# Linear attention, a channel mix and a gated mix in one kernel: plain split products in place of Strassen's, and a list scheduler's order

## The chip, the cores and the metric

The kernel runs on one core of a Trainium2 chip. The time is the device time of one execution in microseconds, shown as the median of three runs. A profile is one more execution with the hardware profiler on; its span runs from the first to the last instruction. TensorE multiplies into PSUM (eight banks), VectorE (DVE) and ScalarE (ACT) read and write PSUM and SBUF, GpSimd (POOL) works on SBUF, and SyncE (SP) issues the DMAs. Each engine takes its instructions in order.

## The reference, cut to what matters

All inputs are float32 or float64 arrays; batch B = 2, heads H = 8, sequence S = 768, head width 64, model width 512.

```
# 1 attention with decay, per head: state = gamma*state + k_t v_t^T ; y_t = scale * q_t state
# 2 token mix of rank 32 and channel mix
xt = x.transpose(0, 2, 1)
u  = x + (xt @ U @ V).transpose(0, 2, 1)
x  = u + np.maximum(u @ w_ch1, 0) @ w_ch2            # 512 -> 2048 -> 512
# 3 gated mix
h    = np.maximum(x @ w_in, 0)                       # 512 -> 1024
u, v = h[..., :512], h[..., 512:]
v_n  = (v - mean(v)) / sqrt(var(v) + 1e-6)           # over the 512 features
v_s  = einsum('ts,bsd->btd', w_spatial, v_n) + b_spatial[None, :, None]
out  = (u * v_s) @ w_out                             # 512 -> 512
```

The weights U, V, w_ch1, w_ch2, w_in and w_out reach the kernel as float64 words and are turned into float32 on the chip.

## The kernel before, in words

**Numbers.** A product of full float32 quality is made of three products of split operands. Each operand is a high part (rounded by ScalarE to the product's type) and the remainder (a subtraction on VectorE or GpSimd): high x high, high x low, low x high (`mm3`, all recorded under L129). An activation block is 128 features x 384 tokens, half of the sequence T = 384. X[b] holds the 512 features of a batch as four tiles of 128 partitions x 768 tokens.

**Attention** goes over eight units i, a pair of heads each (four pairs for batch 0, then four for batch 1), in chunks of 128 tokens. `scale_q`, `scale_k` apply decays. `s1(i)` makes the score products (two heads side by side on half of the array each, tile `sc`), their masking into `pt` (VectorE, or ScalarE and GpSimd), the chunk products k^T v (`ds`) and the running state `s` (VectorE, L226 to L228: ten small steps on the two diagonal blocks of a 128 x 128 tile whose other blocks are zero). `s2(i)` multiplies the states and the probabilities into `x` and copies it to X. `s3`, `s4`, `s5` do the token mix of rank 32: transposes (`t`), their split (`xtok`), the product with U (`g`, twelve products of 256 columns for two pairs), the product with V (`hu`) and the addition to X. These functions are called in an order written out by hand, the later steps of a unit behind the first steps of the next ones.

**Channel mix and gate** use Strassen's scheme in Winograd's form (`strassen`): four output blocks from seven products instead of eight. It needs sums of activation blocks (`form_diff`, L300; split by `form_split`, L292), sums of weight blocks (`sums1`, `sums2`, L472 to L478) and sums of product banks (`y`, L578 to L581, L645). The 2,048 inner features go in eight blocks m of 256: `ch1(m, b)` is one such quad with relu, `ch2(m, b)` multiplies its two inner tiles by w_ch2 into eight banks, and each bank is added to X by VectorE (L674). `ch1` of one block is woven with `ch2` of the block before. `mixu`, `mixv`, `mixo` are the gate's two halves and the output product, with Strassen; `norm` normalises v; `mixs` is the spatial product, plain, its bank multiplied into X (L758, L759). `mixv` and `mixo` have banks of 128 tokens x 256 columns, the others 128 x 384.

**Weights.** `load_next` loads a tile of 128 x 512 float64 words (512 KB) into one of two raw buffers. `conv_a` and `conv_b` make float32 of the words: two ScalarE operations (L366, L367), two on VectorE (L372, L373), one on GpSimd (L374); then the split. A small task queue (`pump`) starts and advances these steps at beats of the program.

**Order.** All instructions are issued in program order; some 300 choices found for this kernel (`CHOICES`: how many tasks begin at a beat, which engine takes a step, orders of products) set where a step stands.

The heart of the scheme:

```
order = pick(f"or{ycls(name)}", order)          # "1675243"
...
    elif x == "6":
        prod(qb, P6, True)
        nc.vector.tensor_add(y1, qb, y1)
    elif x == "7":
        prod(qc, P7, True)
        nc.vector.tensor_add(y2, qc, y1)
```

Of the kernel before, what the change touches and what calls it, by code (L numbers as in the profile page):

```python
# [10 lines left out]
U64 = mybir.dt.uint64  # L11
# [8 lines left out]
DFF2 = 1024  # L20
# [8 lines left out]
NM = NF // 2  # L29
# Beats (how many tasks begin), engines (A, V, G), orders of products and of steps, by point of the program.  # L30
CHOICES = {
# [54 lines left out]
def pick(key, default):  # L86
    """The schedule's choice at a point of the program, where it differs from the usual one."""
    return CHOICES.get(key, default)
# [986 lines left out]
```

## Time and profile before

| | |
|---|---|
| time, three runs | 532.05, 534.75, 538.35 us (median 534.75) |
| span of the profiled execution, first to last instruction | 530.7 us (the profile gives no other time of that execution) |
| TensorE busy, products | 479.1 us (90%), 3,157 |
| VectorE busy, instructions | 439.5 us (83%), 821 |
| ScalarE busy, instructions | 255.4 us (48%), 537 |
| GpSimd busy, instructions | 292.3 us (55%), 265 |
| mean granted TensorE clock | 0.957 of 2.4 GHz |
| HBM read, written | 39.79 MB, 3.15 MB |

Busy shares are means over the whole span. A matmul's length in the profile reaches from its start to the end of its results; successive ones overlap, so rates are read from the distance of starts. A float32 product of the attention is recorded as two instructions, a split product as one. The granted clock of a stretch is a mean over two levels, 1.2 and 2.4 GHz. The words "idle before" name the time in which an engine had nothing running before an instruction, with what released it.

### The profile page before, as it was taken

The page shows a single profiled execution, that of the slowest core. Times are in us where ns is not written, and L with a number is a line of the kernel's source. Part 1 is how long each engine was busy: PE and PEld are TensorE (multiplying, and loading weights), DVE is VectorE, ACT ScalarE, POOL GpSimd, SP SyncE. Part 2 cuts the span into 40 slices and gives each one's busy share as a digit, 9 for nine tenths or more (in the row PEclk, how much of TensorE's full clock was granted, in tenths as well). Part 3 has the DMA queues.
Part 4 walks back from the last instruction along what each step waited for, and adds up shares of the span by engine and source line. Part 5 has one row for each costly group of instructions (what it writes and reads, how often), then busy time and mean ns, then how long its engine had stood idle before and what let it go on. Part 6 is the DMA issues. An engine that isn't in the chain of part 4 may idle for free.

```text
span 530.7 us, 8624 instructions
## 1 busy us (share of the span) xinstructions
PE 479.1 (90%) x3157; PEld 456.0 (86%) x3157; DVE 439.5 (83%) x821; ACT 255.4 (48%) x537; POOL 292.3 (55%) x265
## 2 busy tenths in 40 slices
PE   6878778989888999999999999995899999999697
PEld 4667667979887999999999999883799889999697
DVE  3788899997978987697877878999986886799873
ACT  1575655535454555444544545355343664445220
POOL 2566865683595456554664544676744550476720
PEclk7988898999999999999999999996799999999799
DMA  7996220102322222102222111220001210200123
GB/s 262 315 345 242 93 81 1 41 1 79 120 79 81 80 79 79 50 32 81 79 81 79 51 67 46 78 69 30 1 0 62 90 46 35 80 0 1 40 97 105
DMA packets 17419, 43.50 MB, mean 82 GB/s; under 512 B 2144, under 2 KB 6880, under 8 KB 17376
## 3 DMA queue, kind: packets, MB, share of 16 engines
q1 hardware_dynamic: 17376, 42.94, 24.3%
q8 instruction: 25, 0.41, 0.3%
q14 instruction: 18, 0.15, 0.1%
HBM read 39.79 MB, written 3.15 MB: 81 GB/s over the span
## 4 chain that ended last, share of the span: by engine, by line
PE 47%; DVE 32%; ACT 6%; DMA 6%; issue 5%; POOL 3%; SPq 1%; POOLq 0%; DVEq 0%; ACTq 0%
PE acc L129 17%; DVE t L300 3%; DMA q<-in_qT 3%; DVE x L674 2%; DVE s L228 2%; DVE fb L292 1%; DVE sm L722 1%; DVE pz L758 1%; DMA rawV<-in_V 1%; ACT r L736 1%; DVE x L759 1%; DVE rw L372 1%; DMA k<-in_kT 1%; DVE rw L373 1%; DVE ft L292 1%
## 5 line engine op out<-in xcount | busy, mean ns | idle before, releaser
L129 PE MATMUL acc<-a,hw 128*128 128x384 f32 x512 | 130.6, 335 | 2.0 <-DVE x L674 0.9
L129 PEld LDWEIGHTS acc<-a,hw 128*128 128x128 f32 x512 | 92.3, 188 | 3.2 <-DVE x L674 1.4
L129 PE MATMUL acc<-a,lw 128*128 128x384 f32 x256 | 85.6, 334 | 0.0
L674 DVE TENSOR_TENSOR x<-acc,x 128x384 f32<-128x384 f32 x128 | 68.8, 548 | 6.4 <-PE acc L129 6.4
L156 POOL TENSOR_TENSOR a<-y,a 128x384 fp32r<-128x384 f32 x41 | 42.5, 1042 | 55.4 <-ACT a L155 54.0
L374 POOL TENSOR_TENSOR rw<-rw,tw 128x512 int32<-128x512 int32 x32 | 41.2, 1287 | 47.5 <-DVE rw L373 28.8
L653 ACT ACTIVATE y<-y 128x384 f32<-128x384 f32 x42 | 22.1, 525 | 72.9 <-DVE y L645 72.9
L292 POOL TENSOR_TENSOR ft<-t,ft 128x384 fp32r<-128x384 f32 x33 | 37.6, 1149 | 30.0 <-ACT ft L288 29.8
L129 PEld LDWEIGHTS acc<-a,lw 128*128 128x128 f32 x256 | 48.0, 188 | 0.0
L288 ACT CAST ft<-t 128x384 fp32r<-128x384 f32 x48 | 23.2, 514 | 34.2 <-DVE t L300 34.2
L372 DVE TENSOR_SCALAR rw<-yw 128x512 uint32<-128x512 uint32 x32 | 28.6, 895 | 8.8 <-ACT yw L366 7.4
L292 POOL TENSOR_TENSOR fb<-x,fb 128x384 fp32r<-128x384 f32 x26 | 29.3, 1147 | 2.1 <-ACT fb L288 2.1
L373 DVE SCALAR_TENSOR_TENSOR rw<-yw,rw 128x512 uint32<-128x512 uint32 x32 | 26.5, 827 | 1.1
L129 PE MATMUL pz<-ws,vn 128*128 128x384 f32 x144 | 26.5, 335 | 0.1
L382 ACT CAST hw<-rw 128x512 fp32r<-128x512 f32 x16 | 10.0, 623 | 33.8 <-POOL rw L374 33.8
L129 PEld LDWEIGHTS pz<-ws,vn 128*128 128x128 f32 x144 | 25.1, 188 | 0.4 <-DVE vn L156 0.4
L366 ACT ACTIVATE yw<-raww 128x512 f32<-128x512 f32 x32 | 21.3, 667 | 2.3 <-DVE rw L372 2.3
L155 ACT CAST a<-y 128x384 fp32r<-128x384 f32 x42 | 21.6, 513 | 1.3
L367 ACT ACTIVATE tw<-raww 128x512 int32<-128x512 uint32 x32 | 21.1, 661 | 0.0
L129 PE MATMUL sc<-q,k 64*128 64x128 f32 x192 | 16.8, 324 | 4.3 <-DVE q L194 1.5
L129 PEld LDWEIGHTS sc<-q,k 64*128 64x128 f32 x192 | 14.7, 228 | 6.7 <-DVE q L194 2.7
L288 ACT CAST fb<-x 128x384 fp32r<-128x384 f32 x36 | 17.3, 512 | 4.9 <-DVE x L759 4.8
(1376 smaller groups left out, 1429.2 us busy)
## 6 DMA issues: line engine op xcount, KB each, us to landing
raww<-in_w SPq DMA_DIRECT2D x32, 512.0 KB, 3.6
kk<-in_k SPq DMA_DIRECT2D x8, 384.0 KB, 5.9
v<-in_v SPq DMA_DIRECT2D x8, 384.0 KB, 6.7
out_y<-o SPq DMA_DIRECT2D x24, 128.0 KB, 1.7
q<-in_qT SPq DMA_DIRECT2D x7, 384.0 KB, 5.9
k<-in_kT SPq DMA_DIRECT2D x7, 384.0 KB, 5.7
rawws<-in_ws SPq DMA_DIRECT2D x6, 384.0 KB, 3.1
rawwu<-in_wu SPq DMA_DIRECT2D x4, 512.0 KB, 4.0
```

What stands on the lines that cost most here:

```text
L129: nc.tensor.matmul(o, l, r, start=start, stop=stop, skip_group_check=True)
L155: nc.scalar.copy(hi, raw)
L156: eng.tensor_sub(lo, raw, f(hi))
L288: nc.scalar.copy(t[:, 0, :], blk[o])
L292: E(pick(f"f{b}{k}{o}{blks_gen[0]}", "V" if eng is V else "G")).tensor_sub(t[:, 1, :], blk[o], f(t[:, 0, :]))
L366: nc.scalar.activation(y, words[:, :, 1].bitcast(F32), AF.Copy, scale=2.0 ** -112)
L367: nc.scalar.activation(t, words[:, :, 0], AF.Copy, scale=2.0 ** -29)
L372: nc.vector.tensor_single_scalar(r, y.bitcast(U32), 3, ALU.logical_shift_left)
L373: nc.vector.scalar_tensor_tensor(r, y.bitcast(U32), 0x80000000, r, ALU.bitwise_and, ALU.bitwise_or)
L374: E(pick(f"cv{mcls(nm)}", "G")).tensor_tensor(r.bitcast(I32), r.bitcast(I32), t, ALU.add)
L653: nc.scalar.activation(y, y, AF.Relu)
L674: nc.vector.tensor_add(x, acc, x)
```

## The change

Strassen's scheme is gone: `ch1`, `gate_u`, `gate_v` and `final` are plain sums over four input tiles, three split products each (`triple`). The first channel product has eight products where there were seven; gate v and output make one bank of 128 tokens x 512 columns where there were 256 columns. The inner features go in four blocks of four tiles (GM = 4) instead of eight of two, so a bank of the second channel product sums twelve products instead of six and is added to X half as often. The state of the attention is kept as one 128 x 64 tile per chunk (both heads below each other, five steps instead of ten), and its product with q is two quarter-array products. Only one batch's channel mix begins before the other batch's attention: `AT0`, `AT1`, `CH0`, `CH1` give each step a key, the place that it would have in time in us. q and k are loaded in halves.

No step is issued where it stands in the program. `Plan.op` notes each with its key, the engines that could take it with a duration each, and what it reads and writes. `arrange` then goes through all steps: for each engine it takes, among the steps whose inputs are ready about as early as any (`SLACK`), the one with the lowest key, and gives buffers of the pools (`POOLS`: 36 tiles "a", 30 "w", 2 raw, 8 banks) in the order of the keys. `give_out` issues the result.

```diff
+    LAG = {"P": 198.0, "V": 35.0, "A": 35.0, "G": 35.0, "D": 30.0}
...
+        for _ in order:
+            best = None
+            for e in self.ENGINES:
+                can = []
+                for o in cands[e]:
+                    t0 = room(o)
+                    if t0 is not None:
+                        can.append((o.seq, o, t0) + span(o, e, t0))
...
+                low = min(c[3] for c in can) + SLACK[e]
+                for _, o, t0, st, en in sorted(can, key=lambda c: c[0]):
+                    if st > low:
+                        continue
+                    if any(span(o, x, t0)[1] + BIAS[x] < en + BIAS[e] for x in o.eng if x != e):
+                        continue
+                    if best is None or st < best[0]:
+                        best = st, en, o, e
+                    break
...
+def pe(n, passes=1):
+    return passes * (10.8 + 0.4219 * n), False
+GM = 4
+NM = NF // GM
+POOLS = {"a": 36, "w": 30, "raw": 2, "y": 2, "t": 2, "r": 3, "s": 3, "sm": 2, "ps": 8}
+SLACK = {"P": 30.0, "V": 60.0, "A": 60.0, "G": 100.0, "D": 30.0}
+BIAS = {"V": 300.0, "G": 0.0, "A": 0.0}
+AT0, AT1, CH0, CH1 = 5.0, 42.0, 36.0, 24.0
...
+    def triple(o, start, stop, n, wh, wl, xh, xl, r, flip=False):
...
+                mm(o.t, wh(), xh(), start, False)
+                mm(o.t, wh(), xl(), False, False)
+                mm(o.t, wl(), xh(), False, stop)
+        op({"P": pe(n, 3)}, run, r=r, w=[o])
...
+    def ch1(b, h, i):
+        o = rows(f"c{b}{h}{i}", 0, "w1", i, b, h)
+        A[b, h, i] = t = Buf("a", [P, 2, T], F32R, f"a{b}{h}{i}")
+        op({"A": aps(T)}, lambda E: E.activation(t.t[:, 0, :], o.t, AF.Relu), r=[o], w=[(t, 0)])
+        op({"V": (560, False)}, lambda E: E.scalar_tensor_tensor(t.t[:, 1, :], o.t, 0.0, f(t.t[:, 0, :]), ALU.max, ALU.subtract), r=[o, (t, 0)], w=[(t, 1)])
+
+    def ch2(m, b, h, d):
...
+        for i in range(GM * m, GM * m + GM):
...
+            triple(o, i == GM * m, i == GM * m + GM - 1, T, ...)
+        op({"V": vps(T)}, lambda E: E.tensor_add(xs(b, d, h), o.t, xs(b, d, h)), r=[o, ("X", b, d, h)], w=[("X", b, d, h)])
...
+        grp = 12 * pe(T)[0] / 1000
+        at = [AT0 + 6.5 * i for i in range(NP)] + [AT1 + 9.0 * i for i in range(NP)]
+        for i in range(2 * NP):
+            load_qk(i, at[i] - 12)
...
+            load_kv(i, at[i] - 10)
+        weight_u(at[2] + 3)
...
+        t = CH0
+        for m in range(NM):
+            for b in range(B):
+                ch[m, b] = t
+                t += 16 * grp + (CH1 if (m, b) == (0, 0) else 0)
+        gu = t
+        for m in range(NM):
+            for i in range(GM):
+                weight("w1", GM * m + i, ch[m, 0] + i * grp - LEAD)
...
+        for b in (0, 1):
+            for what in ("uv", "vu")[b]:
...
+        for b in range(B):
+            for h in range(2):
+                for d in range(ND):
+                    spatial(b, h, d)
+                    plan.key += 1.5 * grp
+                    operand(2, b, d, h)
+        for b in range(B):
+            for c in range(NCH):
+                final(b, c)
+                plan.key += 12 * pe(DM)[0] / 1000
+        plan.arrange(POOLS)
```

## Rows read from the trace of the kernel before

**Rows 1.** Stretches: length, TensorE, loads, VectorE, ScalarE, GpSimd busy (instructions), clock, DMA, GB/s.

```profile
0.00:45.00 45.00, 34.53 (x355) 27.23 (x357) 30.62 (x74) 20.23 (x43) 22.27 (x28) 0.85 0.91 306
45.00:93.00 48.00, 38.01 (x400) 32.22 (x396) 44.74 (x98) 29.13 (x65) 32.40 (x29) 0.93 0.24 83
93.00:180.00 87.00, 78.04 (x440) 74.96 (x439) 76.45 (x124) 44.19 (x89) 56.55 (x47) 1.00 0.19 64
180.00:330.00 150.00, 150.00 (x867) 150.00 (x866) 121.13 (x205) 72.10 (x140) 78.65 (x69) 1.00 0.21 69
330.00:390.00 60.00, 48.45 (x235) 44.54 (x234) 57.86 (x87) 28.76 (x61) 41.40 (x35) 0.86 0.12 40
390.00:465.00 75.00, 72.75 (x489) 71.13 (x488) 57.97 (x146) 39.59 (x96) 29.71 (x34) 1.00 0.16 55
465.00:510.00 45.00, 40.08 (x249) 39.15 (x249) 40.30 (x68) 17.91 (x40) 29.13 (x26) 0.92 0.07 24
510.00:525.00 15.00, 14.95 (x124) 14.70 (x124) 9.20 (x22) 3.15 (x8) 2.17 (x2) 1.00 0.33 106
```

**Rows 2.** Timeline of TensorE, 49 to 67 us: start, length, operation, idle time before it.

```profile
49.51 0.88 PE L129 MATMUL x<-pt,v 128*64 128x128 f32 x12
...
53.47 0.80 PE L129 MATMUL ds<-v,kk 128*64 128x64 f32 x20
54.20 0.87 PE L254 MATMUL t<-shared,x 128*128 128x128 f32 x6
54.91 0.61 PE L129 MATMUL x<-q,s 128*128 128x128 f32 x4
55.45 0.88 PE L129 MATMUL x<-pt,v 128*64 128x128 f32 x12
56.26 0.94 PE L129 MATMUL x<-q,s 128*128 128x128 f32 x6
57.12 0.88 PE L129 MATMUL x<-pt,v 128*64 128x128 f32 x12
57.93 0.39 PE L129 MATMUL g<-xtok,ust 128*128 128x256 f32 x1
61.88 2.71 PE L129 MATMUL g<-xtok,ust 128*128 128x256 f32 x11 [3.57 <-DVE xtok L256]
64.53 1.82 PE L129 MATMUL sc<-q,k 64*128 64x128 f32 x24
66.28 0.80 PE L129 MATMUL ds<-v,kk 128*64 128x64 f32 x20
```

**Rows 3.** Timeline of the end of the span: last product and last VectorE instruction.

```profile
527.01 0.28 PE L129 MATMUL qo5d<-hwo3c,fb 128*128 128x256 f32 x1
...
527.33 0.42 DVE L771 TENSOR_TENSOR o<-qo5d,yo 128x256 f32<-128x256 f32 x1 [0.29 <-PE qo5d L129]
```

**Rows 4.** Groups of instructions by line: count, busy us, mean ns, idle time before.

```profile
L129 PE MATMUL acc<-a,hw 128*128 128x384 f32 x512 | 130.6, 335 | 2.0 <-DVE x L674 0.9 <-DVE y L645 0.8 <-POOL a L156 0.3
...
L674 DVE TENSOR_TENSOR x<-acc,x 128x384 f32<-128x384 f32 x128 | 68.8, 548 | 6.4 <-PE acc L129 6.4
...
L366 ACT ACTIVATE yw<-raww 128x512 f32<-128x512 f32 x32 | 21.3, 667 | 2.3 <-DVE rw L372 2.3
...
L372 DVE TENSOR_SCALAR rw<-yw 128x512 uint32<-128x512 uint32 x32 | 28.6, 895 | 8.8 <-ACT yw L366 7.4 <-POOL lw15c L386 1.4
...
L373 DVE SCALAR_TENSOR_TENSOR rw<-yw,rw 128x512 uint32<-128x512 uint32 x32 | 26.5, 827 | 1.1
...
L374 POOL TENSOR_TENSOR rw<-rw,tw 128x512 int32<-128x512 int32 x32 | 41.2, 1287 | 47.5 <-DVE rw L373 28.8 <-ACT tw L367 15.1 <-PE acc L129 3.5
...
L228 DVE SCALAR_TENSOR_TENSOR s<-s,scales,ds 64x64 f32<-64x64 f32 x64 | 17.9, 280 | 2.1
...
L186 ACT ACTIVATE kk<-kk,scales 128x384 f32<-128x384 f32 x16 | 9.0, 615 | 10.2 <-DMA kk<-in_k 10.2
```

**Rows 5.** Waits of TensorE: us in total, times, longest.

```profile
PE qo0a L129 <- DVE yo L575: 4.4, 1, 4.4
```

More of the change, by code (lines that the diff above doesn't have):

```diff
@@ L1 @@
+import heapq
 from contextlib import ExitStack
@@ L19 @@
 DFF = 2048
-DFF2 = 1024
 R = 32
@@ L28, with __init__ @@
 TC = NCH // 2
-NM = NF // 2
-CHOICES = {
[51 rows of a table removed]
-}
-def pick(key, default):
-    return CHOICES.get(key, default)
-WARM = 11
-VIA = {i: (1, 3) for i in range(2, 8)}
-NW = 25
-EPS = 1e-6
-P1, P6, P7, P5 = ("a11", "b11"), ("s2", "t2"), ("s3", "t3"), ("s1", "t1")
-P2, P4, P3 = ("a12", "b21"), ("a22", "t4"), ("s4", "b22")
+EPS = 1e-6
+class Buf:
+    def __init__(self, pool, shape, dt, name):
+        self.pool, self.shape, self.dt, self.name = pool, shape, dt, name
+        self.t, self.left, self.end, self.order = None, 0, 0.0, None
@@ L101, in tile_kernel @@
+BIAS = {"V": 300.0, "G": 0.0, "A": 0.0}
+WARM = 11
+AT0, AT1, CH0, CH1 = 5.0, 42.0, 36.0, 24.0
+LEAD = 25.0
+VIA = {i: (1, 3) if i >= 2 else () for i in range(2 * NP)}
 @with_exitstack
@@ L204, in s1, with run @@
+        ds = bank([P, NCH - 1, D], f"ds{i}")
+        def run(_):
+            for c in range(NCH - 1):
                 for e in range(2):
                     r = slice(64 * e, 64 * e + 64)
[L206 to L215 removed]
@@ L246, in s3, with cpy, turn @@
+    def cpy(e, o, i):
+        (e.copy if e is nc.scalar else e.tensor_copy)(o, i)
+    def turn(i):
         b, p = divmod(i, NP)
@@ L268, in s5, with run @@
-    def s5(i):
+                xtok[j, h] = [Buf("a", [P, TC, 2 * P], F32R, f"xtok{j}{h}{y}") for y in range(2)]
+            hi, lo = xtok[j, h]
+            tr = bank([P, TC, P], f"t{i}{h}")
+            def run(_, tr=tr, h=h):
+                for c in range(TC):
+                    nc.tensor.transpose(tr.t[:, c, :], X[b][:, p, (TC * h + c) * P:(TC * h + c + 1) * P], ident)
+            op({"P": (TC * 111, False)}, run, r=[("X", b, p, h), "ident"], w=[tr])
+            sl = slice(w * P, (w + 1) * P)
@@ L525, in begin @@
-    def begin(stages, tasks):
-        tasks.append(list(stages))
-        advance(tasks, len(tasks) - 1)
-    def pump(n=1, w=0, hold=False):
-        advance(flow)
-        if not hold:
-            advance(wflow)
-        for z in range(n + w):
-            if jobs and z < n:
-                begin(jobs.pop(0), flow)
-                continue
-            if hold or begun[0] == limit[0] or running[0] == most[0]:
-                return
-            if not nxt:
-                t = next(wtasks, None)
-                if t is None:
-                    return
-                nxt.append(t)
-            need, pair, stages = nxt[0]
-            if strict[0] and need > free[0] - sum(x[0] for y in wflow for x in y if isinstance(x, tuple)):
-                return
-            if pair and heavy[0]:
-                return
-            nxt.pop()
-            ends = [end_task]
-            if pair:
-                heavy[0] = True
-                ends = [heavy_end, end_task]
-            running[0] += 1
-            begun[0] += 1
-            begin(stages + ends, wflow)
@@ L679, in weave @@
-    def weave(gens, pattern, beat):
-        for g in pattern:
-            next(gens[g])
-            beat()
-    def mixu(m, b):
-        def store(i, h, src, add=None, y=None):
-            if add is not None:
-                nc.vector.tensor_add(y, src, add)
-                src = y
-            if pick(f"ur{m}{b}{i}{h}", "A") == "A":
-                nc.scalar.activation(X[b][:, 2 * m + i, h * T:(h + 1) * T], src, AF.Relu)
-            else:
-                nc.vector.tensor_single_scalar(X[b][:, 2 * m + i, h * T:(h + 1) * T], src, 0.0, ALU.max)
-            if (b, i, h) == (1, 0, 1):
-                free[0] += 7
-        yield from strassen(f"u{m}{b}", T, ys3(f"u{m}{b}"), rows("wu", m, b), store)
@@ L699, in tile_kernel @@
-    vn, rv, vs = {}, {}, []
-    def mixv(g):
-        b, c = divmod(g, TC)
-        r = [st([P, DM], F32, f"r{g}{h}") for h in range(2)]
-        def store(i, h, src, add=None, y=None):
-            if add is not None:
-                nc.vector.tensor_add(y, src, add)
-                src = y
-            nc.scalar.activation(r[h][:, i * 2 * P:(i + 1) * 2 * P], src, AF.Relu)
-            if (i, h) == (0, 1):
-                vs.append(norm(g))
-        rv[g] = r, psm.tile([P, 2, 16], F32, tag="sm", name=f"sm{g}", bufs=2)
-        yield from strassen(f"v{g}", DM // 2, ys2(f"v{g}", pw, "w"), cols("wv", b, c * P), store, copy=nc.vector.tensor_copy)
@@ new lines, in final, with busy, run @@
+    def final(b, c):
+        o = chunk(f"o{b}{c}", 2, "wo", b, c)
+        t = Buf("w", [P, DM], F32, f"out{b}{c}")
+        op({"A": aps(DM), "V": vps(DM)}, lambda E: cpy(E, t.t, o.t), r=[o], w=[t])
+        dma(lambda: out[b, c * P:(c + 1) * P, :], lambda: t.t[:], P * DM * 4, r=[t])
+    with tc.manual_schedule():
+        warm = nc.const_aps.tensor(1.0, (P, T), BF16)
+        nc.scalar.activation(psm.tile([P, 1], F32, name="table"), warm[:, 0:1], AF.Copy)
+        idle = bank([P, T], "idle")
+        def busy(n):
+            def run(_):
+                for _ in range(n):
+                    mm(idle.t, warm[:, 0:P], warm, True, True)
+            op({"P": (n * 320.0, False)}, run, w=[idle])
+        plan.key = 0.0
+        busy(WARM)
+        grp = 12 * pe(T)[0] / 1000
+        at = [AT0 + 6.5 * i for i in range(NP)] + [AT1 + 9.0 * i for i in range(NP)]
+        for i in range(2 * NP):
+            load_qk(i, at[i] - 12)
+            if i == 0:
+                dma(lambda: ident, lambda: a["ident"], P * P * 4, w=["ident"], key=at[0] - 10)
+            load_kv(i, at[i] - 10)
+        weight_u(at[2] + 3)
+        weight_v(0, at[2] + 3.1)
+        weight_v(1, at[2] + 3.2)
+        for i in range(2 * NP):
+            plan.key = at[i] - 2
+            scale(i)
+            plan.key = at[i]
+            scores(i)
+            plan.key = at[i] + 5
+            mix(i)
+            plan.key = at[i] + 7
+            turn(i)
+            if i % 2:
+                plan.key = at[i] + 8
+                down(i // 2)
+                plan.key = at[i] + 9
+                up(i - 1)
+                up(i)
+        ch = {}
+        t = CH0
[7 more added lines that the diff above has]
+                weight("w1", GM * m + i, ch[m, 0] + i * grp - LEAD)
+            for i in range(GM):
+                weight("w2", GM * m + i, ch[m, 0] + (8 + i) * grp - LEAD)
+        for i in range(ND):
+            weight("wu", i, gu + i * grp - LEAD)
+        for i in range(ND):
+            weight("wv", i, gu + 8 * grp + i * 2 - LEAD)
+        for b in range(B):
+            plan.key = at[NP * b + NP - 1] + 9.5
+            for h in range(2):
+                for k in range(ND):
+                    operand(0, b, k, h)
+        for m in range(NM):
+            for b in range(B):
+                plan.key = ch[m, b]
+                for h in range(2):
+                    for i in range(GM * m, GM * m + GM):
+                        ch1(b, h, i)
+                        plan.key += grp
+                for h in range(2):
+                    for d in range(ND):
+                        ch2(m, b, h, d)
+                        plan.key += grp
+                if m == NM - 1:
+                    for h in range(2):
+                        for k in range(ND):
+                            operand(1, b, k, h)
+        plan.key = t = gu
+        for b in (0, 1):
+            for what in ("uv", "vu")[b]:
+                for h in range(2):
+                    if what == "u":
+                        for i in range(ND):
+                            gate_u(b, h, i)
+                            plan.key += grp
+                    else:
+                        gate_v(b, h)
+                        plan.key += TC * 12 * pe(DM)[0] / 1000
+        t = plan.key
+        for i in range(NCH):
+            weight_s(i, t - LEAD - 10 + 2.0 * i)
+        biases(t - 20)
+        for i in range(ND):
+            weight("wo", i, t + 30 + 2.0 * i - LEAD)
+        plan.key = t
+        for b in range(B):
+            for h in range(2):
+                for d in range(ND):
+                    spatial(b, h, d)
+                    plan.key += 1.5 * grp
+                    operand(2, b, d, h)
+        for b in range(B):
+            for c in range(NCH):
+                final(b, c)
+                plan.key += 12 * pe(DM)[0] / 1000
+        plan.arrange(POOLS)
+        plan.give_out({"P": None, "V": nc.vector, "A": nc.scalar, "G": nc.gpsimd, "D": nc.sync}, pools)
@@ L1042, in ftiles @@
         return raw(x.reshape(ND, P, n, P).transpose(2, 1, 0, 3).reshape(n, P, DM))
-    def halves(x):
-        return raw(x.reshape(2, 2, P, 2, 2 * P).transpose(1, 3, 2, 0, 4).reshape(ND, P, DM))
     return {
```

1058 lines of the change are left out of this document (365 added, 693 removed), and 51 rows, old and new, of the table CHOICES.

## The prediction

> **What bounds the kernel now.** I read the span by stages first, because the page's shares (TensorE 90%, VectorE 83%) are means over stages that have different limits. The stages [rows 1] show three kinds of time. From 180 to 330 us TensorE is busy all 150 us at the full 2.4 GHz: 867 products in 150 us, 0.173 us each for 384 columns. VectorE has 29 us to spare there. From 0 to 93 us (attention) TensorE is busy 72.5 us, at a granted clock of 0.85 and 0.93, and VectorE 44.7 of the last 48. From 93 to 180, 330 to 390 and 465 to 510 us TensorE idles 9.0, 11.6 and 4.9 us while VectorE is busy 88, 96 and 90%. There Strassen's sums are formed: they save TensorE one product in eight and are paid by VectorE.
>
> How far the 90% is from a bound is better counted than read. Dense products of 384 columns: 672 (first channel product) + 768 (second) + 168 (gate's u) + 288 (spatial) = 1,896 at 0.173 us [rows 1] = 328.0 us. Products of 256 columns: 252 + 252 = 504 at 0.1206 us (124 in 14.95 us at full clock, last row of [rows 1]) = 60.8. Attention, from the starts on TensorE [rows 2]: state products 0.73, transposes 0.71, outputs 0.54 + 0.81 + 0.86 + 0.81, scores 1.75 (64.53 to 66.28, partly at a lower clock, so a ceiling): 6.2 us a pair of heads, eight pairs 49.7. The 48 + 16 low-rank products come to about 8.6 at the dense rates. Together 447 us of work in a span of 530.7: 84 us are idle time, half clock and the warm-up products. About 35 us of it lie in the first 93 us (93 - 58 of attention), 19 from 330 to 390 (235 products are 41 us of work), 11 from 93 to 180 and 5 from 465 to 510.
>
> **The change, part by part.**
>
> *Plain products.* The first channel product goes from 672 to 768 products and the gate's u from 168 to 192: 120 x 0.173 = **+20.8 us**. The gate's v and the output go from 504 products of 256 columns to 288 of 512 columns. Width 512 is not in the trace. A line through 256 and 384 columns gives 0.225 us, twice the 256 row gives 0.241; I take 0.226, nearest the wider row: 65.1 us, **+4.3** (up to +8.6). Dense work after: 2,016 x 0.173 + 65.1 = **413.9 us**.
>
> *What leaves VectorE.* Five sums a quad (32 quads), the 48 sums of activation blocks and the sums of weight blocks go. The second channel product sums four blocks in PSUM instead of two, so its 128 additions at 0.548 us [rows 4] become 64. What is left on VectorE: 64 additions and 64 relu remainders at 0.55 = 70; conversions 44 x (0.895 + 0.827) = 76 [rows 4]; masks, states, transposes and low-rank additions 42; spatial and norm 34. That is 222 us, and at most 230 on GpSimd even if it took every remainder. GpSimd's share of a conversion is 1.29 us [rows 4]. ScalarE: 44 weights at 2 x 0.667 [rows 4] + a copy, operands, relus and attention, about 227. All are under half of a 500 us span, so from the point where dense work can start TensorE is the bound, as it is from 180 to 330 us now. I cost these removals at nothing of their own: they count only through the idle time that goes.
>
> *Where dense work can start.* Batch 0's four pairs must be through the low-rank mix. Its input is 4 x 1.5 MB; with two of the small matrices and four weight tiles (0.5 MB each) queued between, about 9.4 MB at 306 GB/s [rows 1] is landed by about 31 us. The last pair then goes through kk scaling 2 x 0.615, state products 0.73, five state steps at 0.28 [rows 2, 4], outputs 3.0, copy, transpose 0.4, split, 12 low-rank products 1.45, the up products, an addition and a split: about 14 us. So **45 us** at the earliest without waiting. VectorE has about 32 us of work and ScalarE 33 in the 42 us since the first scores, which costs a little; I take **47 us**. Lower end 41 (weights loaded behind the attention, part of the chain overlapped). Upper end 57: in the kernel before, pair 3's last output products start at 49.51 [rows 2] and end at about 50.5, and 6.5 us of chain follow.
>
> *Batch 1's attention beside batch 0's channel mix.* Its TensorE work stays: 4 x 6.2 + two low-rank products (2.9) + up (1.6) = 29.3 us, but its waits, VectorE's and ScalarE's, are now covered by 33 us of dense products of the same stretch. What would be uncovered if that cover failed is a rival below. The state product with the compact state is two quarter-array products instead of one full one; not in the trace. If the two run side by side it costs what five full ones cost (1.4 us a pair), if not, 2.7; I take 1.4, as score pairs do run side by side, and keep +5 us for the range.
>
> *Shape changes.* Now half-array and full-array products alternate product by product. The row pair: two state-output products after a full-array transpose take 0.54, three after a half-width one 0.86 [rows 2], 0.27 and 0.29 each, so a change costs about 0.05 us. If a change cost all of the overlap between one product and the next, it would be 0.335 - 0.173 = 0.16 us [rows 1, 4]. Seven attention steps a pair, two changes each, four pairs: 56 changes, 2.8 to 9.0 us; I take 4, nearer the row that shows changes. The Trainium skill (TensorEngine Tiling (Array Packing), Key Properties) speaks against the alternation: changing the tiling mode, not just the tile, drains TensorE. The row pair does not show a full drain; by that rule the sum would come out 5 us higher.
>
> *Stalls and queues.* The order on each engine is fixed by the list scheduler from its own durations, and every queue is in order: a product with a late operand holds all products behind it. From 390 to 465 us, where VectorE is 77% busy, TensorE idles 2.25 of 75 us; from 180 to 330 none. After, VectorE is less loaded than in either. I take 6 us for the 450 us that follow, between 0 and 3% = 13. SP's queue issues q and k in halves, two issues more a pair; a weight load waits there for one of two raw buffers, with attention loads behind it: that is in the 41 to 57 above. The 8 PSUM banks hold a sum longer, but a sum of twelve products takes 2.1 us and its eviction 0.55, so three banks suffice.
>
> *Tail.* After the last product starts (527.01) the span runs 3.7 us [rows 3]. The last copy is now 512 columns wide with one 256 KB store: 3.9.
>
> *Sum.* 47 + 413.9 + 29.3 - 4 (products on blocks that are ready before 47 us, six banks' worth at most) + 4 + 6 + 3.9 = **500 us of span**. The profiled span of before is 530.7, its runs 532.05 to 538.35, median 534.75: 1.4 to 4 us more than the span. With 4 on top: **504 us**, 30 us or 6% less than the median. The low end: start 41, no stalls, changes at 2.8, 1.4 on top: 488. The high end: start 57, stalls 13, and half of the dearer ends of the 512-column and compact-state products (4.6): 526.
>
> **The rivals.**
>
> *The cover fails.* Batch 1's attention holds up the order instead of hiding in it: 36 tile buffers must carry its loads, probabilities and token copies beside the channel mix's operands and results, and the planner's priorities may simply put it ahead, so that the change doesn't overlap what it says. Against: in that stretch there are 33 us of dense work on tiles already split. For: in the kernel before, state products of successive pairs start at 53.47 and 66.28 [rows 2], 12.8 us a pair against 6.2 of work. Four pairs then lose 4 x 6.6 = 26 us: 530, within 1% of before. Half of it gives 517, inside the range.
>
> *Slower than before.* Operands late at block boundaries. There are twelve: four blocks times two batches, two gates, the spatial and the output product. Each block's operands come from a VectorE addition, a ScalarE copy and a remainder of VectorE or GpSimd, 2.3 us. If the fixed order puts the first product of a block before its remainder is there, TensorE idles and then runs at half clock: the low-rank product waited 3.57 us and its next eleven products took 2.65 us instead of 1.33 [rows 2], 4.9 us a boundary; the output product waited 4.4 us for VectorE in the same way [rows 5]. All twelve cost 59 us less the 6 already counted: 557. It decides from nine boundaries up (over 540). Against: two batches alternate, so 33 us of the other batch's products lie between a batch's last addition and its next product, and VectorE has half its load gone.
>
> *Nearly no loss.* The scheduler fills the start with batch 1's pairs and dense products on the first two pairs: start-equivalent 36, no stalls: 483.
>
> **How the numbers follow.** The forecast with its range holds 0.80, the failed cover at its full price (about 530) 0.06, the late boundaries 0.07, nearly no loss 0.05; 0.02 I leave to effects that no row shows. So the range is 488 to 526 and leaves out about 2 in 10. Under 1% a measurement of this kernel, whose three runs span 1.2%, can't be told from no change; 1% faster is 529.4, 1% slower 540.1. Faster: 0.80 + 0.05 + a third of the failed cover = 0.87. Slower: 0.07 and the unseen. Same: the rest.
>
> **What would show it.** Right: TensorE busy without gaps at full clock from about 50 us to the end, 29 us of attention products between dense ones; products of 512 columns about 0.226 us apart; VectorE near 45 to 55% busy; the chain of waits almost all TensorE. Wrong start: the first long run of first-channel products after 57 us. Failed cover: TensorE idle between 47 and 105 us, waiting for masks, states or loads. Late boundaries: idle time before the first product of a block, released by a remainder, with the clock below full behind it. If GpSimd or ScalarE is over 80% busy in any 50 us stretch while TensorE waits, the claim that TensorE alone bounds it is wrong.

## The result, and the profile after

The changed kernel takes **516.65 us** (median of four runs, 516.16 to 516.86), the kernel before, run beside it, 533.65: a ratio of 0.9656 [0.96, 0.9712]. That is 3.4% faster, inside the range of 488 to 526, and 12.65 us above the 504 that were forecast. The profiled execution took 516.86 us with a span of 515.1. That span is 15.6 us shorter than the 530.7 of before: TensorE has 24.3 us less idle time (27.3 against 51.6, each span less TensorE's busy time) and 8.7 us more busy time (487.8 against 479.1).

The stages of the changed kernel, with the columns of [rows 1]:

```profile
0.00:45.00 45.00, 32.17 (x387) 24.38 (x387) 28.65 (x61) 23.32 (x46) 13.37 (x16) 0.84 0.77 275
45.00:93.00 48.00, 37.60 (x271) 33.81 (x272) 37.98 (x63) 29.86 (x62) 24.39 (x21) 0.79 0.55 177
93.00:180.00 87.00, 86.44 (x652) 83.14 (x652) 64.34 (x110) 46.38 (x88) 36.68 (x29) 1.00 0.32 104
180.00:330.00 150.00, 150.00 (x867) 150.00 (x867) 75.63 (x124) 44.89 (x84) 23.00 (x18) 1.00 0.13 41
330.00:390.00 60.00, 60.00 (x334) 58.17 (x333) 24.57 (x45) 24.12 (x47) 8.27 (x7) 1.00 0.19 61
390.00:465.00 75.00, 75.00 (x404) 71.19 (x403) 42.58 (x97) 31.06 (x58) 1.29 (x1) 1.00 0.02 6
465.00:510.00 45.00, 45.00 (x219) 39.62 (x218) 8.97 (x16) 9.09 (x17) 0.00 (x0) 1.00 0.15 59
```

From 93 us on the idle time of [rows 1] is gone: 9.0, 11.6, 2.3 and 4.9 us have become 0.6, 0, 0 and 0. VectorE, 77 to 96% busy in those stages before, is at 74% from 93 to 180 us and under 60% afterwards. Ahead of 93 us the idle time did not shrink: TensorE is busy 69.8 us of the first 93 against 72.5 before, and at a lower clock from 45 us on (0.79 against 0.93). What TensorE waited for (us in total, times, longest):

```profile
PE g L248 <- POOL ust L457: 9.5, 1, 9.5
PE hu L248 <- POOL vst L463: 6.2, 2, 4.9
...
PE c L248 <- DVE f L417: 0.4, 1, 0.4
```

And where these waits stand on TensorE's timeline (start, length, operation, idle time before it):

```profile
37.93 1.19 PE L380 MATMUL t<-shared,x 128*128 128x128 f32 x6
48.64 5.49 PE L248 MATMUL g<-xtok,ust 128*128 128x256 f32 x24 [9.52 <-POOL ust L457]
59.02 1.65 PE L248 MATMUL hu<-vst,gt 128*128 128x384 f32 x4 [4.89 <-POOL vst L463]
62.00 1.65 PE L248 MATMUL hu<-vst,gt 128*128 128x384 f32 x4 [1.34 <-POOL vst L463]
63.45 0.52 PE L248 MATMUL c<-f,hw 128*128 128x384 f32 x1
```

Batch 0's attention is over at 39 us. Then the low-rank mix stands still, first for U (`ust` is its split form), then for each half of V (`vst`). The first product of the channel mix (`c`) starts at 63.45 us, where 47 was forecast and 57 the latest. Two other engines show why. SyncE's queue, the DMA issues, and what the queue waited for between 30 and 40.5 us:

```profile
25.55 1.23 SPq L254 DMA_DIRECT2D raww<-in_w  x2
...
30.33 0.33 SPq L254 DMA_DIRECT2D v<-in_v  x1
40.13 0.33 SPq L254 DMA_DIRECT2D rawU<-in_U  x1
41.63 4.00 SPq L254 DMA_DIRECT2D rawV<-in_V  x5
...
48.96 0.43 SPq L254 DMA_DIRECT2D rawV<-in_V  x1
```

```profile
SPq L254 <- ACT tw L438: 7.7, 1, 7.7
SPq L254 <- DMA raww<-in_w: 1.8, 1, 1.8
```

ScalarE, the conversions of the raw words, and the second copy of the low-rank product (`gt`):

```profile
38.89 0.66 ACT L437 ACTIVATE yw<-raww 128x512 f32<-128x512 f32 x1
39.45 0.66 ACT L438 ACTIVATE tw<-raww 128x512 int32<-128x512 uint32 x1
...
43.73 0.36 ACT L437 ACTIVATE yU<-rawU 128x192 f32<-128x192 f32 x1
...
54.16 0.37 ACT L398 CAST gt<-g 128x256 fp32r<-128x256 f32 x1 [2.19 <-PE g L248]
54.63 0.54 ACT L437 ACTIVATE yV<-rawV 128x384 f32<-128x384 f32 x1
```

Two weight tiles, issued at 25.55, hold both raw buffers until ScalarE converts them from 38.89 on. In the order that the scheduler fixed, U's load stands behind them: SyncE issues nothing between 30.7 and 40.13 us, then U goes out 0.02 us after the first tile's second conversion ends (40.11). Of these 9.5 us the first 1.8 are the tile's landing; the other 7.7 pass with the tile landed, while ScalarE's order has attention steps ahead of its conversion. V comes next, each half in four pieces, one behind another, because every piece is planned as a write of the same whole buffer; the last piece is issued at 48.96, and the longest landing of a piece is 4.2 us. The first conversion of V starts later still, at 54.63: the copy `gt` stands ahead of it in ScalarE's order, and that copy waited for the products with U. So part of V's lateness is U's.

### The profile page after: what moved, and what is told of

The parts are those of the page before. It is cut to its first block, busy times and chain, and to the rows that moved or that the text cites. A ratio compares the mean times of both kernels' runs of the same rounds, so it can differ in the third digit from the quotient of the medians.

```text
span 515.1 us, 7732 instructions
## 1 busy us (share of the span) xinstructions
PE 487.8 (95%) x3131; PEld 461.3 (90%) x3131; DVE 282.7 (55%) x514; ACT 209.3 (41%) x399; POOL 107.0 (21%) x89
## 4 chain that ended last, share of the span: by engine, by line
PE 91%; DVE 4%; DMA 1%; ACT 1%; SPq 1%; POOL 1%; issue 0%; POOLq 0%
PE acc L248 26%; PE c L248 25%; PE pz L248 10%; PE u L248 6%; PE o L248 6%; PE v L248 6%; PE x L248 5%; PE sc L248 2%; PE g L248 2%; DMA v<-in_v 1%; PE ds L248 1%; PE t L380 1%; DVE rw L440 1%; SPq L254 1%; DVE pt L327 1%; DVE f L417 1%
## 5 line engine op out<-in xcount | busy, mean ns | idle before, releaser
L248 PE MATMUL c<-f,hw 128*128 128x384 f32 x512 | 132.2, 338 | 0.5 <-DVE f L417 0.4
L248 PEld LDWEIGHTS c<-f,hw 128*128 128x128 f32 x512 | 92.9, 189 | 1.8 <-DVE f L417 1.4
L248 PE MATMUL c<-f,lw 128*128 128x384 f32 x256 | 86.1, 336 | 0.0
L506 ACT ACTIVATE a<-c 128x384 fp32r<-128x384 f32 x64 | 31.4, 491 | 95.7 <-PE c L248 95.5
L516 DVE TENSOR_TENSOR x<-acc,x 128x384 f32<-128x384 f32 x64 | 35.6, 555 | 48.2 <-PE acc L248 48.2
L507 DVE SCALAR_TENSOR_TENSOR a<-c,a 128x384 fp32r<-128x384 f32 x64 | 35.1, 554 | 45.3 <-ACT a L506 45.0
L248 PEld LDWEIGHTS c<-f,lw 128*128 128x128 f32 x256 | 48.5, 189 | 0.0
L248 PE MATMUL u<-f,hwu 128*128 128x384 f32 x128 | 32.5, 334 | 0.0
L248 PE MATMUL v<-hwv,f 128*128 128x512 f32 x96 | 29.8, 389 | 0.0
L248 PE MATMUL o<-hwo,f 128*128 128x512 f32 x96 | 29.7, 389 | 0.0
L447 ACT CAST hw<-rw 128x512 fp32r<-128x512 f32 x32 | 19.3, 617 | 16.7 <-PE acc L248 11.1
```

The costliest lines, as they stand in the source:

```text
L248: nc.tensor.matmul(o, l, r, start=start, stop=stop, skip_group_check=True)
L447: op({"A": acp(DM)}, lambda E: E.copy(h.t, r.t.bitcast(F32)), r=[r], w=[h])
L506: op({"A": aps(T)}, lambda E: E.activation(t.t[:, 0, :], o.t, AF.Relu), r=[o], w=[(t, 0)])
L507: op({"V": (560, False)}, lambda E: E.scalar_tensor_tensor(t.t[:, 1, :], o.t, 0.0, f(t.t[:, 0, :]), ALU.max, ALU.subtract), r=[o, (t, 0)], ...
L516: op({"V": vps(T)}, lambda E: E.tensor_add(xs(b, d, h), o.t, xs(b, d, h)), r=[o, ("X", b, d, h)], w=[("X", b, d, h)])
```

## The experiments

All edits are against the changed kernel unless said otherwise. Each is timed beside the kernel before.

**What holds the start? U's place in the order.** U and V get earlier planned times, ahead of the first-channel weight tiles.

```
-        weight_u(at[2] + 3)            # at[2] = 18
-        weight_v(0, at[2] + 3.1)
-        weight_v(1, at[2] + 3.2)
+        weight_u(10.0)
+        weight_v(0, 10.1)
+        weight_v(1, 10.2)
```

> The changed kernel with one edit: the keys of the low-rank matrices U and V are 10.0 to 10.2 instead of 21.0 to 21.2, so that they come before the first four weight tiles in the order. In the changed kernel TensorE idled 9.5 us before the first low-rank product (for U) and 6.2 us before the second one (for V), and the first channel product started at 64.4 us. Theory A (U and V are late because they wait for a raw buffer behind two weight tiles): both waits go, the first channel product starts near 48 us and the time is 500 to 505. Theory B (V is late for itself: each of its two halves is loaded in four pieces that the plan puts one behind the other, because all four are noted as writing the same buffer): the wait for U goes, the wait for V stays and the first weight tiles are late instead; 512 to 520.

518.89 us (518.09 to 519.73): not faster, as theory B said. (The first channel product of the changed kernel starts at 63.45 us; 64.4 is the start of its second.) The waits:

```profile
PE hu L248 <- POOL vst L463: 6.7, 2, 5.7
PE c L248 <- DVE a L507: 6.4, 1, 6.4
PE c L248 <- DVE f L417: 2.6, 2, 2.3
```

The wait for U is gone, so its place was what made it. V's stays, and the time saved on U turns up later, as 6.4 us of first-channel products behind a VectorE remainder (`a`) and 2.6 behind the split of their tokens (`f`). A cause that is truly there can be taken away without moving the end.

**V's serial pieces.** Each piece becomes a buffer part of its own for the planner; both conversions read all four.

```
-        for dst, src in load(raw):
-            dma(dst, src, ..., w=[raw], key=key - 14)
+        parts = [(raw, x) for x in range(len(load(raw)))]
+        for part, (dst, src) in zip(parts, load(raw)):
+            dma(dst, src, ..., w=[part], key=key - 14)
...
-        op({"A": c}, ... r=[raw], w=[y])
+        op({"A": c}, ... r=parts, w=[y])
```

> The changed kernel with one edit: the four pieces in which a half of V is loaded are noted as writing four parts of the raw buffer, so that the plan issues them side by side; the keys stay. Theory A (the raw buffer is what U and V wait for): the wait of 9.5 us for U stays, the one for V shortens; the first channel product at 58 to 62 us, 510 to 515. Theory B (the pieces of V are the cause): the wait for V is gone and the first channel product comes right behind the low-rank products that now start at 48.6 us, at 56 us: 508.

514.88 us (514.22 to 515.89), in theory A's range by the time. The first channel product comes at 55.22 us, earlier than theory A's 58 to 62 and near theory B's 56; an 8.2 us earlier start has given 1.8 us. The waits:

```profile
PE g L248 <- POOL ust L458: 9.7, 1, 9.7
PE hu L248 <- DVE gt L399: 3.8, 1, 3.8
...
PE hu L248 <- POOL vst L464: 1.7, 1, 1.7
```

The wait for V falls from 6.2 to 1.7 us, but 3.8 us of it are replaced by the step before on the same chain (`gt`, the copy of the first low-rank product).

**Both.**

> Both edits: V's pieces side by side and the keys of U and V ahead of the first weight tiles. Theory A and B together (the late start is the whole difference to the forecast of 504): no wait for U or V, the first channel product at 45 to 50 us, 499 to 505. Rival C (the next thing is late instead: the weight tiles of the first channel product now come behind U and V through the same two raw buffers, ScalarE, VectorE and GpSimd): the first channel product starts early but TensorE idles between its products up to 65 us; 507 to 512.

511.88 us (510.9 to 513.75), as rival C said. No wait for U or V is left among the larger ones:

```profile
PE c L248 <- DVE f L417: 2.1, 2, 1.3
PE g L248 <- DVE xtok L384: 1.9, 1, 1.9
...
PE hu L248 <- DVE gt L399: 1.5, 1, 1.5
PE sc L248 <- DVE x L408: 1.4, 1, 1.4
```

The first-channel products begin at 48.65 us, near the forecast's 47, and yet only 4.8 us are gained: from 38 to 65 us TensorE is busy 18.80 of 27 us, waiting in many small pieces for token copies, splits and weight halves, and VectorE is busy 24.98 of the same 27. So the 16.5 us by which the start came late were not all U's and V's to give back; something has to fill TensorE while the chain of batch 0 goes through VectorE.

**Is the overlap worth anything?** Batch 1's attention is planned directly behind batch 0's, and both channel mixes behind that; the planned times of U and V are those of the changed kernel.

```
-AT0, AT1, CH0, CH1 = 5.0, 42.0, 36.0, 24.0
+AT0, AT1, CH0, CH1 = 5.0, 31.0, 67.0, 0.0
```

> The changed kernel with the overlap undone and nothing else: batch 1's attention has the keys 31 to 58 and the channel mix starts at key 67, so that all of the attention comes before the first channel product, as in the kernel before. Theory D (the overlap is worth what it covers): batch 1's four pairs run uncovered at 10.8 to 12.8 us each behind a start like the one of now, the first channel product comes at about 105 us with 414 us of dense products behind it: 524 or more. Theory E (batch 1's attention only fills idle time, here the hole of 26 us that TensorE has from 38 to 64 us while it waits for U and V, and the order of the two stretches does not matter): first channel product at 90 to 97 us, 510 to 518, no more than 5 us from the changed kernel.

510.67 us (509.79 to 513.92): theory D falls. Theory E has the time and the first channel product (90.46 us), though 6 us are a little more than its 5. In the profiled execution, the slowest of the four (513.92), TensorE still waits 8.3 us for V, but no longer for U, whose load goes out early:

```profile
13.04 0.43 SPq L254 DMA_DIRECT2D rawU<-in_U  x1
```

So the edit does more than undo the overlap. The weight tiles' planned times hang on the channel mix's, and with that at 67 they no longer stand ahead of U. The 6 us are not the overlap's alone. A closer pair is this run and the first experiment, which has the overlap, an early U (5.43 us) and V's pieces serial: 518.89 against 510.67, 8.2 us. Attention that is ready fills the hole in which the channel mix had nothing to multiply.

**Is the rest bound by TensorE alone?** Three edits. First, sums of six products again instead of twelve (`GM = 4` to `GM = 2`).

> The second channel products are summed over six products in PSUM again instead of twelve, so VectorE makes twice as many additions into the accumulator there (some 64 more by about 0.34 us = 22 us of VectorE). Theory F (after the start TensorE alone sets the pace, and VectorE at 55% has room): within 2 us of the changed kernel's 516.6, and the 15 us windows from 135 us on hold 14.9 us or more of TensorE. Rival G (the longer sums were needed to keep VectorE from holding up PSUM buffers): 520 to 535, with waits of TensorE for those additions.

511.76 us (511.46 to 512.41): faster than either theory said. The 64 additions more are there (VectorE 308.6 us busy against 282.7), and from 135 to 420 us TensorE has no idle time, as theory F said. The gain comes from the front, where the scheduler's order came out another way: U's load is issued at 25.85 us instead of 40.13.

```profile
PE hu L248 <- POOL vst L463: 7.0, 2, 5.6
...
PE g L248 <- POOL ust L457: 1.5, 1, 1.5
```

That the earlier U made the gain is read from this trace, not isolated. From the first channel product to the last product this run takes 452.1 us (53.74 to 505.83) against 447.8, with 2.0 us of waits for batch 1's tokens at 109 to 111 us that the changed kernel does not have. So the longer sums are worth nothing after 120 us; whether they help ahead of that, where the order differs too, this run can't tell.

Second, 64 products fewer.

```
-                mm(o.t, wl(), xh(), False, stop)
+                if not two:                  # two: kind == "w1" and k == ND - 1
+                    mm(o.t, wl(), xh(), False, stop)
```

> Leaves out one of the three products of the last 128 rows in each first channel sum (low half of the weight by high half of the tokens): 64 of 2,016 products with 256 columns. Theory F (TensorE alone sets the pace, 0.1733 us a product): 64 x 0.1733 = 11.1 us less, so 504.5 to 506.5. Rival H (a good part of the dense stretch is set by something beside TensorE): 2 to 7 us less, 509 to 515, with new waits of the first channel products for operands or PSUM buffers.

505.52 us (505.35 to 506.56): 11.13 us less, where 64 x 0.1733 is 11.1. (The products left out have 384 columns, not 256; 0.1733 is the price of 384.) The first-channel products count in full.

Third, the VectorE remainder of each activated tile (`a`) made twice.

> The VectorE instruction that makes the low half of each activated first channel tile is issued twice with the same result: 64 more by about 0.55 us = 35 us of VectorE, all in the dense stretch of the two batches. Theory F (VectorE has room and its work is hidden behind the products): within 2 us of 516.6. Rival G (the activated tile is needed at once, or VectorE's queue holds up the attention steps beside it): 2 to 20 us more, with TensorE waiting for VectorE at the first or second channel products.

516.17 us (515.84 to 517.78): 0.5 us less, no difference, with 24.6 us more of VectorE (GpSimd took some steps over: 114.3 us against 107.0). Theory F stands for the channel mix, where both edits lie.

**All attention first, with U and V early.** V's pieces as above, and (LEAD is how far ahead of its first product a weight tile is planned):

```
-AT0, AT1, CH0, CH1 = 5.0, 42.0, 36.0, 24.0
-LEAD = 25.0
+AT0, AT1, CH0, CH1 = 5.0, 24.0, 67.7, 3.4
+LEAD = 15.0
-        at = [AT0 + 6.5 * i ...] + [AT1 + 9.0 * i ...]
-        weight_u(at[2] + 3)                   # V: + 3.1, + 3.2
+        at = [AT0 + 7.3 * i ...] + [AT1 + 5.8 * i ...]
+        weight_u(13.3)                        # V: 13.4, 13.5
```

> U and V loaded and split earlier, V's pieces loaded side by side, the attention of both batches one after the other at the front, closer together, and the dense products behind it. Theory (what is lost after the change is the 17 us by which the dense stretch starts late, and attention needs no dense products beside it): 490 to 502, first channel products beginning late but TensorE with little idle time before them, and no wait of several us for U, V or their halves. Rival I (attention without dense work beside it runs at its chain of waits, at half clock, as in the first 45 us): 505 to 520, with TensorE's idle time spread over many short waits of g, x and sc for VectorE and GpSimd.

**492.63 us** (491.77 to 493.14), ratio to the kernel before 0.9203 [0.9169, 0.9237]: it beats both kernels, the changed one by 24 us. Its stretches:

```profile
15.00:30.00 15.00, 14.13 (x184) 10.89 (x180) 9.81 (x23) 8.02 (x18) 5.82 (x7) 0.92 1.01 360
30.00:45.00 15.00, 15.00 (x233) 13.03 (x231) 11.19 (x28) 10.04 (x21) 9.75 (x11) 1.00 0.95 325
45.00:60.00 15.00, 15.00 (x200) 12.49 (x198) 12.35 (x30) 12.65 (x29) 10.63 (x11) 1.00 0.41 138
60.00:75.00 15.00, 15.00 (x167) 13.51 (x162) 14.37 (x33) 12.49 (x28) 5.14 (x6) 1.00 0.25 76
```

TensorE has no idle time from 30 us to its last product, at full clock. The channel mix starts at 69.53 us, later than in the changed kernel, and that costs nothing, since by then both batches' attention is done but for the last transposes and low-rank products. Of the 24.3 us of span between the two, 17.3 are idle time (27.3 against 10.0, each span less TensorE's busy time) and 7.0 are busy time (487.8 against 480.8 for the same 3,131 products), most of it products at half clock. The attention of two batches covers itself: rival I falls. (It also misread the front: the first 45 us of the changed kernel were granted 0.84, well above half clock.)

**Its parts, put back.** The smaller LEAD and the distances of the pairs stay as they are in all three runs. The overlap (`AT0, AT1, CH0, CH1 = 5.0, 42.0, 36.0, 24.0` again):

> The version with all attention first (492.6 us), with only the overlap put back: batch 1's attention and the first channel products get the planned places that they have in the changed kernel, while U and V stay early and V's pieces side by side. Theory K (the overlap is worth nothing by itself, and it moves work into the front where operands and weight tiles aren't there yet): 500 to 510, with short waits of the first channel products for VectorE's splits and for weight tiles before 110 us. Rival L (the late U and V alone made the loss, the overlap is neutral): 490 to 496.

508.28 us (507.65 to 509.37). Stretches and waits:

```profile
30.00:45.00 15.00, 13.22 (x162) 10.19 (x160) 12.74 (x26) 10.64 (x23) 8.63 (x8) 1.00 1.03 365
45.00:60.00 15.00, 11.87 (x91) 10.04 (x91) 14.33 (x22) 12.10 (x25) 8.72 (x8) 1.00 0.45 155
60.00:75.00 15.00, 10.76 (x66) 8.82 (x66) 10.78 (x20) 8.36 (x15) 9.67 (x7) 0.83 0.41 140
```

```profile
PE c L248 <- ACT hw L448: 2.6, 3, 1.1
PE x L248 <- DVE s L339: 2.3, 3, 1.5
PE x L248 <- DVE s L341: 2.2, 1, 2.2
...
PE c L248 <- DVE lw L449: 1.2, 2, 0.7
PE c L248 <- POOL lw L449: 1.0, 1, 1.0
```

9.2 us of TensorE go between 30 and 75 us, in waits for weight halves (`hw`, `lw`) and state steps: dense products were planned where their weight tiles were not yet split. VectorE is 96% busy from 45 to 60 us, 6.0 of 14.3 us with weight tiles and 5.3 with splitting tokens. It is 15.6 us slower than without the overlap. Theory K is in its range. The weight tiles have a LEAD of 15 here and batch 1's pairs are 5.8 us apart, where the changed kernel has 25 and 9.0, so not all planned places are the changed kernel's; but "Both" above, which has the changed kernel's values, was no faster (511.88).

V's pieces serial again:

> The version with all attention first (492.6 us), with only V's pieces chained one behind another again. Theory M: V comes some 5 us later; as V is loaded at the start, 30 us before its first product, this costs 0 to 3 us: 492 to 496. Rival O (SyncE's queue stands still at each piece, and the loads of q, k and v for the first pairs stand behind it): 497 to 506, with waits of TensorE for the loads of q, k or v before 30 us.

502.5 us (501.89 to 503.33), 9.9 us slower and outside theory M's 492 to 496. The time is rival O's, the mechanism is not: there is no large wait for q, k or v, but

```profile
PE hu L248 <- POOL vst L463: 5.2, 1, 5.2
```

The first half of V, split at 21.2 us in the version before, is split at 57.5: one piece of V goes out at 5.9 us, two at 29.3 and the last five from 38.2 on, with attention loads between, and the conversions were put at 53.7. I had counted only landing times, not that every later step of the order moves with them. Another 1.7 us are waits for weight halves, and TensorE's busy time is 3.4 us longer (484.2 against 480.8).

U's and V's planned times put back:

> The version with all attention first (492.6 us), with only U's and V's planned times put back behind the first weight tiles. Theory M (the raw buffers that they wait for are what holds the front up, with or without the overlap): 500 to 510, and TensorE waits for a half of U or V by 3 to 10 us at about 40 to 60 us. Rival N (with attention of batch 1 to put into the hole, their place doesn't matter): 491 to 496.

495.48 us (494.86 to 496.8), in rival N's range. But the edit did not make what it was to test: with the channel mix planned at 67.7 no weight tile stands ahead of U any more (U's load goes out at 13.05 us, the first weight tile's at 36.76). So neither theory is decided by this run: like the edit that undid the overlap, it moved the weight tiles too. It fits the reading that the planned time of U matters only against the tiles that compete for the two raw buffers. A third raw buffer, the direct test of that, was not tried.

The overlap once more, with planned times chosen for it (`AT1` 37.8, `CH0` 35.8, `CH1` 26.9, `LEAD` 16.6, pairs 8.5 and 6.9 us apart, U and V at 12.5):

> The overlap kept, with the planned times of both batches chosen anew for it: batch 0's pairs 8.5 us apart, batch 1's from 37.8 us on and 6.9 us apart, batch 0's channel mix from 35.8 us, U and V early and V's pieces side by side. Theory K (the overlap brings dense products to a place where their weight tiles and token halves aren't ready, and gives nothing back): 494 to 505, slower than 492.6 with waits of first channel products for weight or token halves before 80 us. Rival P (the overlap itself is neutral, and only its planned times were bad): 489 to 493.5.

496.12 us (495.76 to 496.96): 3.5 us slower than all attention first, with 1.3 us of waits of `c` for weight halves. From 30 to 75 us TensorE idles 1.7 us, where it had no idle time with all attention first. Theory K's range; rival P falls, by a little: the ratios to the kernel before, 0.9277 [0.9236, 0.9318] and 0.9203 [0.9169, 0.9237], just touch. So most of the loss in the first overlap was where it was put. The overlap itself gave nothing in either placing that was tried; another placing may.

## Why the prediction was right, and where it was off

**What bounds the kernel: right.** That TensorE alone sets the pace of the channel mix is what the runs with 64 products fewer and with the remainder made twice show; for the gate and the output it is read from the stages above, where TensorE has no idle time. The idle time that the prediction read at VectorE's busy stretches is gone. How much of that is the plain products' and how much the scheduler's was not tried: no run undid only one of the two, so the cause of the gain is argued here, not shown. VectorE was busy 282.7 us where 222 were counted: the order gave it most remainders of tokens and weights (`f`, `lw`: 58.5 us), which the prediction had left to GpSimd. At 55% of the span that changed nothing.

**Where dense work can start: the mis-sized term.** 47 us were taken, 57 was the latest; it was 63.45, 16.5 us over. The prediction had named the wait (a weight load for one of two raw buffers, with attention loads behind it) and said that it lay within 41 to 57. It did not, and what stood behind the weight tiles was U: 9.52 us for U and 4.89 + 1.34 for V are idle time, and behind them the clock was at half (granted 0.50 from 48 to 54 us), so that 24 low-rank products took 5.49 us (12 take 1.68 to 1.70 at full clock with all attention first: 2.1 us over) and eight up products 3.30 (four take 0.96 to 0.98 there: 1.4 us over). 63.45 less these 19.2 is 44.2, the prediction's "45 us at the earliest without waiting". The upper end came from the kernel before, whose queue has another order: a bound taken from the old order is no bound for a new one. The run with both edits shows that the term was wrong in kind as well: with U and V in time the first dense product starts at 48.65, and some 12 of the 16.5 us are still lost (only 4.8 are gained), because products start before the operands of the following ones exist.

**From the start to the last product: right.** 447.8 us (63.45 to 511.22) against 413.9 + 29.3 - 4 + 4 + 6 = 449.2. The pieces:

- Products of 384 columns 0.1733 us (blocks of 96 in 16.64), of 512 columns 0.227 (144 in 32.68), against 0.173 and 0.226. Dense work is 414.8 by these.
- That leaves 33.0 us for attention, changes of shape, stalls and half clock, forecast 35.3. No dense product stood ahead of the start, so the 4 us taken off for those were wrong; stalls were about 1 us where 6 were allowed. That the two nearly cancel is luck.
- The compact state product was taken at 1.4 us a pair. It takes 1.24 (from the second row below to the third, 82.54 to 83.78).

```profile
82.27 0.34 PE L248 MATMUL c<-f,lw 128*128 128x384 f32 x1
82.54 1.31 PE L248 MATMUL x<-q,s 64*64 64x128 f32 x20
83.78 1.53 PE L248 MATMUL x<-pt,v 128*64 128x128 f32 x24
85.24 0.62 PE L248 MATMUL c<-f,hw 128*128 128x384 f32 x2
85.69 0.34 PE L248 MATMUL c<-f,lw 128*128 128x384 f32 x1
```

- Changes of shape: from 82.27 to the quarter-array product 0.27 us pass where 0.173 is normal, and back, two products take 0.45 instead of 0.35. So a change costs about 0.10 us, between the two ends of 0.05 and 0.16. The Trainium skill (TensorEngine Tiling (Array Packing), Key Properties) says that a change of tiling mode drains TensorE. This trace shows something like two thirds of the overlap of two products lost at a change (0.10 of 0.16), less than the prediction took a full drain to cost. How many changes there were was not counted.

**Tail and outside: small.** From the last product's start to the end of the span 3.9 us, as forecast. Outside the span 1.8 us, where 4 were taken: the 4 had set the span of one execution against the times of others.

The sum: +16.5 - 1.4 + 0 - 2.2 = +12.9, for 516.9; the profiled run took 516.86. The start lay outside its own bounds (41 to 57) and the time still inside the range, because the range's end added several dear terms and only this one came.

**The rivals.** The failed cover was in fact read in the wrong place: attention beside dense work ran almost without waits (14.4 to 15.0 of every 15 us from 75 us on), and the loss came ahead of it. That half of the failed cover gives 517, next to the 516.65 measured, is luck. Late boundaries did not occur after 135 us. "Nearly no loss" (483) is what the all-first version (492.63) comes nearest to, by another order: not by filling the front with dense products but by leaving them out of it.

**What should have shown it blind.** The scheduler's edit gives U a planned time behind the weight tiles, the pool has two raw buffers, and the first users of those are tiles not needed until the channel mix. All of it could be read from the diff; the term was sized from the old trace instead of being followed through the new queue.

## What to carry to other kernels

When a change brings a new order of loads, follow the first user of each scarce buffer through the new queue, step by step; a bound from the old trace does not hold for it. Overlapping two stages gains only if the second stage's operands are ready in the hole that it is to fill: here the attention of the other batch was ready and dense products were not, and leaving the overlap out was worth 8.2 us with V's pieces serial, 15.6 with loads in time, and 3.5 against an overlap with planned times chosen for it. Taking one wait away may move nothing (U's and V's place alone) while a like edit together with others is part of 24 us (all attention first), so test the parts of a front-end chain together as well as alone.

## What the hardware showed that was not expected

Idle time in the front is paid twice. The changed kernel's stretch 45 to 60 us was granted a mean of 0.61 of 2.4 GHz, between its two levels of 1.2 and 2.4; its first dense products are 0.32 us apart until 67 us, and 0.17 apart again from 69.4 on, where the clock was back at full. In the version without idle time from 30 us on, the same 3,131 products took 7.0 us less.

Quarter-array state products take less than half the time each, as they would if two ran side by side: 20 instructions with 128 columns take 1.24 us, 0.062 each, against 0.14 for each of the ten full-array instructions of [rows 2] that they replace (4 from 54.91 to 55.45 us, 6 from 56.26 to 57.12). Twice the instructions, and still 0.16 us less a pair.
